# Cached-attention decode block: one in-order load queue with a rotating ring in place of two queues with two slots each, and another route for the probabilities

## The chip, the cores and the metric

The kernel runs on one core of a Trainium2 chip. The metric is the device time of one execution in microseconds. Before the change three executions took 1314.25, 1317.78 and 1319.87 us; the median is 1317.78 us. The profile is of the first of these, with a span of 1312.3 us from its first to its last instruction.

A core has five engines that run their own instruction streams and meet at semaphores: PE (TensorE, matmul), DVE (VectorE), ACT (ScalarE), POOL (GpSimd) and SP (SyncE). Loads from memory are issued by SP and ACT and carried by the core's 16 DMA engines.

## The reference, cut to what matters

One token for each of 4 sequences goes through an attention block with a cache of 8192 keys and values for each of 32 heads, and then through a gated MLP. Both sit behind a layer norm and a residual.

```python
B, Sq, D = 4, 1, 512
H, Sk, Dh = 32, 8192, 128
...
q = (layernorm(x) @ wq).reshape(B, Sq, H, Dh).transpose(0, 2, 1, 3)
scores = einsum("bhqd,bhkd->bhqk", q, k_cache) * (Dh ** -0.5)
p = softmax(scores, axis=-1)
o = einsum("bhqk,bhkd->bhqd", p, v_cache)
h = x + o.transpose(0, 2, 1, 3).reshape(B, Sq, H * Dh) @ wo
# gated MLP, F = 1792
hn = layernorm(h)
h2 = h + (sigmoid(hn @ w_gate) * (hn @ w_up)) @ w_down
```

All arrays are bf16. The key cache and the value cache are 4 x 32 x 8192 x 128 x 2 bytes = 268 MB each; the weights come to some 14 MB.

## The kernel before

The 128 pairs of sequence and head are the steps of the kernel (NST = 128). One load brings a tile of two heads of K, or of V: 4096 KB, so 64 tiles of each (NT2 = 64). Eight steps make a group (GS = 8, so NG = 16) with one softmax. The values are used LAG = 10 steps behind the keys. A ring of NS = 4 slots in on-chip memory holds the tiles.

**Slots and queues.** K owns slots 0 and 1, V owns slots 2 and 3. At the start slot 3 holds wq, and slot 2 holds a scratch form of the queries ("qr"). `place` notes which tile last held the slot (`prev_of`); a load waits until that tile is `consumed`.

```python
        owner = [None, None, ("qr", 0), None]
        ...
        place(("wq", 0), 3)
        for t in range(NT2):
            place(("k", t), t % 2)
            place(("v", t), 2 + t % 2)
        place(("wg", 0), 0)
        slot_of[("wu", 0)], prev_of[("wu", 0)] = 0, prev_of[("wg", 0)]
        place(("wd", 0), 1)
        ...
        for it in [("wq", 0)] + [("k", t) for t in range(NT2)] + [("wg", 0), ("wu", 0), ("wd", 0)]:
            issue("sp", it)
```

**Keys.** Four VectorE transposes a step turn the tile half of one head (as uint32, 128 x 1024 each), and 16 matmuls add the scores to the group's bank. After its second step a K tile is consumed.

```python
        def dve_T(s):
            ...
                    return e.transpose(kT[:, buf, i * q:(i + 1) * q].bitcast(U32),
                                       ringv(src)[:, base + i * q:base + (i + 1) * q].bitcast(U32))
                op = P("dve", f, [dma_of[it][0], sc_of.get(s - 2)])
            ...
            consumed[it] = op
```

**Softmax of a group.** VectorE takes the row maximum of the scores (`chain_mx`, step 8 after the group's first), PE and VectorE bring it to one row and back (`chain_p1`, `chain_d2`, `chain_p2`, steps 8 and 9), and ScalarE takes the exponential into `E_sb` (128 x 512, bf16) with its sums (`chain_exp`, step 9).

**Probabilities to the key partitions.** This is the first part that the change touches. 64 matmuls of 32 columns each, with a block of `E_sb` as the stationary operand, put the probabilities into a PSUM bank with the keys on the partitions; two ScalarE copies then spread them into `PTz`, a zero-padded tile.

```python
        def chain_pt(g):
            def f(e):
                for rr in range(16):
                    for a in range(4):
                        mm = e.matmul(bP[g % 2][32 * a:32 * (a + 1), 32 * rr:32 * rr + 32],
                                      E_sb[:, 32 * rr:32 * rr + 32], Sel[:, a, :], start=True, stop=True,
                                      tile_position=(0, 32 * a))
                return mm
            pt_of[g] = P("pe", f, [exp_of[g], c_sel] + list(ptc_of.get(g - 2, ())))
            ...
                    src = bP[g % 2][p0:p0 + 64, :].rearrange("p (q r m) -> p q m r", q=4, r=4)
                    return e.activation(dst, src, ACT.Copy)
                ops.append(P("act", fc, [pt_of[g], zp] + last_pv))
```

**Values.** 16 matmuls of 128 x 512 a step take `PTz` as the stationary operand and the V tile as the moving one. They wait for the group's `PTz` and the V tile. A V tile is consumed after its second step.

**Order of a step.** On VectorE a step's four transposes come first, with the softmax pieces between or behind them. On PE come the scores of step s, the pieces of the softmax, the values of step s - 10, and then `chain_pt` where s is 9 past a group's first step. The next V load and, near the end, the eight loads of wo stand on ScalarE at the end of a step:

```python
            t = (s - LAG - 1) // 2 + 2
            if (s - LAG) % 2 == 1 and 2 <= t < NT2:
                for i in wo_after.get(t, ()):
                    issue("act", ("wo", i))
                issue("act", ("v", t))
```

**The end.** wo lies over the buffer of the transposed keys, so its loads wait for the last scores. The last V tile comes in three pieces. Then follow the sum's scaling, the product with wo, the second norm, gate and up (one 1792 KB load each), the hidden vector `hh_sb`, and down (three pieces, 5, 5 and 4 of 14 row blocks), and 4 KB of output. The loads of w_gate, w_up and w_down wait for the values of step 123 too:

```python
        for it, ops in dma_of.items():
            for op in ops:
                op.deps = [sc_of[NST - 1]] if it[0] == "wo" else [consumed[p] for p in prev_of[it]]
                if it[0] in ("wg", "wu", "wd"):
                    op.deps.append(pv_of[NST - 5])
```

Of the kernel before, what the change touches and what calls it, by code (L numbers as in the profile page):

```python
# [5 lines left out]
BF16 = mybir.dt.bfloat16  # L6
# [3 lines left out]
ACT = mybir.ActivationFunctionType  # L10
# [5 lines left out]
LAG = 10  # L16
NS = 4
# [57 lines left out]
def bass_sequential_preLN__mha_block_cached__glu_gated_glu__decode_kernel(  # L75
# [12 lines left out]
    B, _sq, D = A_x.shape  # L88
# [7 lines left out]
    NT2 = NT // 2  # L96
    NST = NT
    NG = NST // GS
    R = S // 64
    TW = R * 128  # L100
# [6 lines left out]
    P = prog.add  # L107

    with ExitStack() as es:
        def SB(name, shape, dt):  # L110
            return es.enter_context(nc.sbuf_tensor(name, shape, dt))
# [12 lines left out]
        Sel = SB("Sel", [128, 4, 32], BF16)  # L124
        SelQ = SB("SelQ", [128, 4, 4], BF16)
# [8 lines left out]
        xT = SB("xT", [128, NDC * B], FP32)  # L134
        xnT = SB("xnT", [128, NDC, 32], BF16)
        E_sb = SB("E_sb", [128, 512], BF16)
        PZ0 = 24
        PTz = SB("PTz", [128, 2, 128 * 32 + 32], BF16)
        mx = SB("mx", [128, 1], FP32)
# [18 lines left out]
        bS, bO, bP = bank[0:2], bank[2:4], bank[4:6]  # L158
        bX, bH = bank[6], bank[7]
# [8 lines left out]
        def ringv(slot):  # L168
            return ring[:, slot, :]
# [2 lines left out]
        VL_PARTS = [(0, 64), (64, 96), (96, 128)]  # L172
        NWO = 8
        HW = H // NWO

        slot_of, prev_of, dma_of, uses = {}, {}, {}, [0] * NS
        owner = [None, None, ("qr", 0), None]

        def place(it, slot):
            slot_of[it] = slot  # L180
            prev_of[it] = [owner[slot]] if owner[slot] is not None else []
            owner[slot] = it
        place(("wq", 0), 3)
        for t in range(NT2):
            place(("k", t), t % 2)
            place(("v", t), 2 + t % 2)
        place(("wg", 0), 0)
        slot_of[("wu", 0)], prev_of[("wu", 0)] = 0, prev_of[("wg", 0)]
        place(("wd", 0), 1)
        consumed = {}  # L190

        wq_v = ring[:, slot_of[("wq", 0)], :].rearrange("p (c f) -> p c f", c=NDC)
# [5 lines left out]
        def kv_src(t, cache):  # L198
# [4 lines left out]
                  sem=s_x, val=16)  # L203
# [40 lines left out]
                dst, src = wu_v, B_w_up.rearrange("(c p) f -> p c f", p=128)  # L244
            return [(lambda e: e.dma_start(dst, src).then_inc(sem, 16), sem, val)]  # L245

        def issue(eng, it):
            dma_of[it] = [P(eng, fn, (), sem, val) for fn, sem, val in load(it)]


        for it in [("wq", 0)] + [("k", t) for t in range(NT2)] + [("wg", 0), ("wu", 0), ("wd", 0)]:
            issue("sp", it)


        def pool(fn, deps=()):
# [70 lines left out]
        consumed[("wq", 0)] = p_q[1]  # L326


        QR0 = 2 * TW
        q_ev = []  # L330
        for half in range(2):
            for a in range(4):
# [9 lines left out]
        def pe_qT(e, half):  # L342
            mm = None
            for h in range(16 * half, 16 * half + 16):
                j = (h // 4) % 4
                for v in range(4):
                    off = half * 2048 + ((h % 4) * 4 + v) * 128
                    c0 = ((h * 4) + v) * 4
                    mm = e.matmul(bX[:, c0:c0 + B], ringv(2)[:, off:off + 128], SelQ[:, j, 0:B], start=True, stop=True)
# [6 lines left out]
        for b in range(B):  # L356
            ops = []
# [22 lines left out]
        z_of, ot_of, otc_of = {}, {}, {}  # L380

        def dve_T(s):
            it = ("k", s // 2)
            src, buf, base = slot_of[it], s % 2, (s % 2) * HT
            q = HT // 4
            op = None
            for i in range(4):
                def f(e, i=i):
# [3 lines that stand above are left out]
                yield  # L392
            T_of[s] = op
            consumed[it] = op
# [82 lines left out]
            d3_of[g] = P("dve", lambda e: e.reciprocal(rinv[:, g % 2:g % 2 + 1], bX[:, 0:1]), [L_of[g], z_of.get(g - 2)])  # L477

        def chain_pt(g):
            def f(e):  # L480
                mm = None
                for rr in range(16):
                    for a in range(4):
                        mm = e.matmul(bP[g % 2][32 * a:32 * (a + 1), 32 * rr:32 * rr + 32],  # L484
                                      E_sb[:, 32 * rr:32 * rr + 32], Sel[:, a, :], start=True, stop=True,
                                      tile_position=(0, 32 * a))
                return mm
            pt_of[g] = P("pe", f, [exp_of[g], c_sel] + list(ptc_of.get(g - 2, ())))
            last_pv = [pv_of[(g - 2) * GS + GS - 1]] if g >= 2 else []
            ops = []  # L490
            for h2 in range(2):
                def fc(e, h2=h2):
                    p0 = 64 * h2

                    dst = bass.AP(PTz, p0 * 2 * 4128 + (g % 2) * 4128 + PZ0 + 4 * h2,
                                  [[2 * 4128, 64], [1024, 4], [32, 32], [1, 4]])
                    src = bP[g % 2][p0:p0 + 64, :].rearrange("p (q r m) -> p q m r", q=4, r=4)
                    return e.activation(dst, src, ACT.Copy)  # L498
                ops.append(P("act", fc, [pt_of[g], zp] + last_pv))
            ptc_of[g] = ops  # L500

        def chain_z(g):
# [14 lines left out]
        def hook(s, base):  # L517
            g = (s - base) // GS
            return g if (s - base) % GS == 0 and 0 <= g < NG else None

        issue("act", ("v", 0))
        issue("act", ("v", 1))
        wo_after = {NT2 - 3: (0, 1), NT2 - 2: (2, 3, 4), NT2 - 1: (5, 6, 7)}


        for s in range(NST + LAG - 2 + 4):
            tr = dve_T(s) if s < NST else iter(())
            for i in range(4):
# [36 lines left out]
            if g is not None and g < NG - 1:  # L565
                chain_ot(g)
            t = (s - LAG - 1) // 2 + 2
            if (s - LAG) % 2 == 1 and 2 <= t < NT2:
                for i in wo_after.get(t, ()):
                    issue("act", ("wo", i))  # L570
                issue("act", ("v", t))


        def wo_mms(e, heads, b0, b1, first=False):
# [8 lines left out]
        gl = NG - 1  # L583
        P("pe", lambda e: wo_mms(e, range(0, H - 8), 0, B, True), [otc_of[gl - 1], dma_of[("wo", NWO - 1)][0], d_xnT])
        if B > 1:
# [15 lines left out]
                                          start=True, stop=True), [d_hsq, c_mean, d3_of[gl]])  # L601
# [45 lines left out]
        p_o = P("pe", lambda e: e.matmul(bP[0][0:NB, 0:128], oT[:, :], ident[:, :], start=True, stop=True),  # L647
                [d_o] + list(ptc_of[gl]) + list(ptc_of[gl - 1]))
        o0 = P("dve", lambda e: e.tensor_copy(o_sb[:, :], bP[0][0:NB, 0:128]), [p_o])
        consumed[("wg", 0)] = consumed[("wu", 0)] = consumed[("wd", 0)] = p_d[-1]  # L650

# [2 lines left out]
            return e.wait_ge(s_out, 16)  # L654
        P("sp", sp_out, [o0])

        for it, ops in dma_of.items():
            for op in ops:
                op.deps = [sc_of[NST - 1]] if it[0] == "wo" else [consumed[p] for p in prev_of[it]]
                if it[0] in ("wg", "wu", "wd"):  # L660
                    op.deps.append(pv_of[NST - 5])

        prog.resolve(sems)
        with nc.Block() as block:
# [47 lines left out]
```

## Time and profile before

| | before |
|---|---|
| median of three executions | 1317.78 us |
| span of the profiled one | 1312.3 us |
| read from memory | 550.77 MB, 420 GB/s over the span |
| VectorE busy | 625.6 us, of which the K transposes 588.2 us |
| PE busy | 473.4 us, mean granted clock 0.649 |
| ScalarE busy | 46.0 us |
| K load, issue to landing | 29.6 us, median of 64 |
| V load, issue to landing | 32.2 us, median of 63 |

How to read the profile. Its first part gives the busy time of each engine, its share of the span and the number of instructions; PEld is the weight load of PE. The second part cuts the span into 40 equal slices of 32.8 us: a digit is the busy share in tenths, and GB/s is what the DMA engines moved. The third lists the queues: packets, megabytes, and the share of the 16 engines' time. Windows give the same for any stretch in us from the span's start: its length, then the busy time (and instructions) of PE, PEld, DVE, ACT and POOL, then the granted clock of PE, the DMA share and GB/s. A window of a few us carries an error of some GB/s, since whole packets are counted. The chain of waits follows the work that ended last back to its start: the start of a piece, its length, and what it was. A DMA piece lasts from its issue to its landing.

### The profile page before, as it was taken

To read this page: it belongs to the slowest core of one execution; us is meant where nothing else is said; L and a number is where in the kernel's file an instruction comes from. 1 tells how busy PE (TensorE), PEld (TensorE's weight loads), DVE (VectorE), ACT (ScalarE), POOL (GpSimd) and SP (SyncE) were. 2 spreads that over 40 slices of the span, in tenths; PEclk is the share of its full clock that TensorE was granted. 3 is DMA by queue.
4 is the path that set the end of the run, shared out by engine and by line. 5 is a ranking of instruction groups with operands and counts; after the bars stand their busy time and mean duration, and the time that the engine had idled before them with its cause. 6 is when DMAs were issued, how large, how long until landed. Compare 5 with 4: busy or idle time off the path is not lost.

```text
span 1312.3 us, 12694 instructions
## 1 busy us (share of the span) xinstructions
PE 473.4 (36%) x5827; PEld 176.8 (13%) x5827; DVE 625.6 (48%) x641; ACT 46.0 (4%) x102; POOL 10.6 (1%) x22
## 2 busy tenths in 40 slices
PE   2134342333333253332334244243243234323324
PEld 1011110111111010110111011011111111111113
DVE  5486455445355355445446445445535436545300
ACT  2000000000000000000000000000000000000000
POOL 3000000000000000000000000000000000000000
PEclk9997556775566656676665655676556665577665
DMA  9999999999999999999999999999999999999895
GB/s 402 432 380 418 434 430 432 430 431 429 430 432 430 431 430 432 431 430 431 429 431 432 431 431 432 431 430 432 428 432 431 430 430 431 431 430 430 356 396 209
DMA packets 26076, 551.58 MB, mean 420 GB/s; under 512 B 2340, under 2 KB 8232, under 8 KB 9256
## 3 DMA queue, kind: packets, MB, share of 16 engines
q1 hardware_dynamic: 12288, 278.14, 49.6%
q10 hardware_dynamic: 13736, 272.64, 48.7%
q8 instruction: 45, 0.74, 0.2%
q14 instruction: 7, 0.06, 0.0%
HBM read 550.77 MB, written 0.00 MB: 420 GB/s over the span
## 4 chain that ended last, share of the span: by engine, by line
DMA 71%; DVE 24%; ACTq 3%; PE 1%; issue 1%; ACT 0%; DVEq 0%
DMA ring<-in_A_k_cache_dram 66%; DVE kT L389 22%; DMA ring<-in_A_v_cache_dram 3%; ACTq L209 2%; DMA ring<-in_A_wq_dram 1%; ACTq L217 1%; DVE mx L445 1%; ACTq L245 0%; PE PS L322 0%; DVE Lq L366 0%; DVE rowx L457 0%; PE PS L624 0%; PE PS L431 0%; DVE mrow L455 0%; DVE ring L339 0%
## 5 line engine op out<-in xcount | busy, mean ns | idle before, releaser
L389 DVE STREAM_TRANSPOSE kT<-ring 128x1024 uint32<-128x1024 uint32 x512 | 588.2, 1209 | 591.1 <-DMA ring<-in_A_k_cache_dram 591.1
L407 PE MATMUL PS<-kT,Lq 128*32 128x512 bf16 x2048 | 217.6, 566 | 773.5 <-DVE kT L389 606.5
L431 PE MATMUL PS<-ring,PTz 128*32 128x512 bf16 x2048 | 210.1, 553 | 33.9 <-DMA ring<-in_A_v_cache_dram 33.6
L407 PEld LDWEIGHTS PS<-kT,Lq 128*32 128x32 bf16 x2048 | 53.9, 119 | 914.8 <-DVE kT L389 673.0
L431 PEld LDWEIGHTS PS<-ring,PTz 128*32 128x32 bf16 x2048 | 64.8, 125 | 132.8 <-issue 81.0
L466 ACT ACTIVATE negm<-PS 128x1 f32<-128x1 f32 x16 | 2.7, 171 | 1157.2 <-PE PS L462 1157.2
L503 DVE TENSOR_SCALAR Zs<-PS,rinv 128x512 f32<-128x512 f32 x16 | 11.6, 724 | 49.4 <-PE PS L431 49.4
L498 ACT ACTIVATE PTz<-PS 64x512 bf16<-64x512 f32 x32 | 18.9, 591 | 18.5 <-PE PS L484 18.1
L510 PE MATMUL PS<-SelZ,Zs 128*128 128x8 f32 x128 | 18.2, 269 | 0.9 <-DVE Zs L503 0.9
L510 PEld LDWEIGHTS PS<-SelZ,Zs 128*128 128x128 f32 x128 | 16.7, 204 | 10.2 <-issue 8.4
L484 PEld LDWEIGHTS PS<-Sel,E_sb 128*32 128x32 bf16 x1024 | 11.3, 100 | 9.1 <-ACT E_sb L468 6.7
L484 PE MATMUL PS<-Sel,E_sb 128*32 128x32 bf16 x1024 | 11.4, 188 | 1.5 <-ACT E_sb L468 1.1
L445 DVE TENSOR_REDUCE mx<-PS 128x1 f32<-128x512 f32 x16 | 10.5, 657 | 1.3 <-PE PS L407 1.2
L468 ACT ACTIVATE E_sb<-PS,negm 128x512 bf16<-128x512 f32 x16 | 11.0, 687 | 0.5
L473 PEld LDWEIGHTS PS<-sig,Gsum 128*128 128x128 f32 x32 | 7.8, 305 | 12.6 <-issue 12.6
L515 DVE CAST OT<-PS 128x8 bf16<-128x8 f32 x16 | 2.1, 132 | 15.5 <-PE PS L510 15.5
L473 PE MATMUL PS<-sig,Gsum 128*128 128x1 f32 x32 | 9.2, 356 | 0.0
L578 PE MATMUL PS<-OT,kT 128*128 128x4 bf16 (+2 forms) x160 | 4.6, 167 | 11.3 <-DMA kT<-in_A_wo_dram 11.0
L462 PE MATMUL PS<-onesf,rowx 1*128 1x1 f32 x32 | 7.5, 300 | 0.0
L462 PEld LDWEIGHTS PS<-onesf,rowx 1*128 1x128 f32 x32 | 6.1, 237 | 9.8 <-issue 9.8
L339 DVE CAST ring<-PS 128x512 bf16<-128x512 f32 x4 | 2.5, 684 | 9.8 <-PE PS L322 9.8
L578 PEld LDWEIGHTS PS<-OT,kT 128*128 128x128 bf16 x160 | 4.4, 103 | 12.2 <-issue 11.9
(78 smaller groups left out, 77.1 us busy)
## 6 DMA issues: line engine op xcount, KB each, us to landing
ring<-in_A_k_cache_dram SPq DMA_DIRECT2D x64, 4096.0 KB, 29.6
ring<-in_A_v_cache_dram ACTq DMA_DIRECT2D x63, 4096.0 KB, 32.2
ring<-in_A_wq_dram SPq DMA_DIRECT2D x1, 4096.0 KB, 12.2
kT<-in_A_wo_dram ACTq DMA_DIRECT2D x8, 512.0 KB, 18.8
ring<-in_A_v_cache_dram ACTq DMA_DIRECT2D x1, 2048.0 KB, 28.3
ring<-in_A_v_cache_dram ACTq DMA_DIRECT2D x2, 1024.0 KB, 21.8
ring<-in_B_w_gate_dram SPq DMA_DIRECT2D x1, 1792.0 KB, 16.2
ring<-in_B_w_up_dram SPq DMA_DIRECT2D x1, 1792.0 KB, 21.8
```

What stands on the lines that cost most here:

```text
L209: return [(lambda e: e.dma_start(wo_v[:, HW * t:HW * t + HW, :], A_wo.rearrange("(h p) f -> p h f", p=128)[:, HW * t:HW * t + HW, :]).then ...
L217: return e.dma_start(ringv(slot)[:, c0:c1], kv_src(t, A_v_cache)[:, c0:c1]).then_inc(s_piece[i], 16)
L389: return e.transpose(kT[:, buf, i * q:(i + 1) * q].bitcast(U32), ringv(src)[:, base + i * q:base + (i + 1) * q].bitcast(U32))
L407: mm = e.matmul(bS[g % 2][32 * j:32 * (j + 1), :], Lq[:, l0:l0 + 32], rhs, start=(s % GS == 0 and v == 0), stop=(s % GS == GS - 1 and v == 3),
L431: mm = e.matmul(bO[g % 2][32 * rq:32 * (rq + 1), :], PTz[:, g % 2, l0:l0 + 32], ringv(slot)[:, r0 * 128:(r0 + 4) * 128], start=(s % GS == ...
L445: mx_of[g] = P("dve", lambda e: e.tensor_reduce(mx[:, :], bS[g % 2][:, :], AX.X, ALU.max), [sc_of[g * GS + GS - 1], p1_of.get(g - 1)])
L462: p2_of[g] = P("pe", lambda e: e.matmul(bX[:, 0:1], rowx[0:1, :], onesf[0:1, 0:1], start=True, stop=True), [d2b_of[g], c_ones])
L473: L_of[g] = P("pe", lambda e: e.matmul(bX[:, 0:1], Gsum[:, :], sig[:, 0:1], start=True, stop=True), [exp_of[g], a1_of[g], d_g])
L484: mm = e.matmul(bP[g % 2][32 * a:32 * (a + 1), 32 * rr:32 * rr + 32], E_sb[:, 32 * rr:32 * rr + 32], Sel[:, a, :], start=True, stop=True, ...
L498: return e.activation(dst, src, ACT.Copy)
L503: z_of[g] = P("dve", lambda e: e.tensor_scalar(Zs[:, :], bO[g % 2][:, :], rinv[:, g % 2:g % 2 + 1], None, op0=ALU.mult), [pv_of[g * GS + G ...
L510: mm = e.matmul(bX[:, 256:264], Zs[:, 128 * r:128 * (r + 1)], SelZ[:, r, :], start=(r == 0), stop=(r == 3))
```

## The change

It has two parts.

The first puts every load on SyncE, in one list: wq, then the first five K tiles, then K and V in turn with V five tiles behind, wo in three portions between the last V tiles, and gate, up and down behind the last V. The slots go round in the order of this list, whatever the kind. It is for a fixed order of the loads, which is the order of use, and it takes the DMA issues and their waits off ScalarE. The extra wait of the last weights is dropped.

The second changes how the probabilities come to the key partitions. Four matmuls of 512 columns gather the rows of `E_sb` (with a selection matrix as the stationary operand), ScalarE copies the result to `Ep`, VectorE transposes it in 32 x 32 blocks to `Et` at the start of the next step, and the two ScalarE copies spread `Et` into `PTz`. It is for fewer PE instructions, and it needs one PSUM bank in place of two.

```diff
+        Ep = SB("Ep", [128, 512], BF16)
+        Et = SB("Et", [128, 512], BF16)
 ...
-        owner = [None, None, ("qr", 0), None]
-        def place(it, slot):
 ...
-        for t in range(NT2):
-            place(("k", t), t % 2)
-            place(("v", t), 2 + t % 2)
 ...
+        LAG2 = LAG // 2
+        items = [("wq", 0)]
+        for t in range(NT2 + LAG2):
+            if t < NT2:
+                items.append(("k", t))
+            if t >= LAG2:
+                items.append(("v", t - LAG2))
+            for i in {LAG2 - 4: (0, 1), LAG2 - 3: (2, 3, 4), LAG2 - 2: (5, 6, 7)}.get(t - NT2, ()):
+                items.append(("wo", i))
+        items += [("wg", 0), ("wu", 0), ("wd", 0)]
+        owner = [None] * (NS - 1) + [("qr", 0)]
+        cur = 0
+        for it in items:
 ...
+            slot_of[it] = cur
+            prev_of[it] = [owner[cur]] if owner[cur] is not None else []
+            owner[cur] = it
+            cur = (cur + 1) % NS
 ...
-        for it in [("wq", 0)] + [("k", t) for t in range(NT2)] + [("wg", 0), ("wu", 0), ("wd", 0)]:
-            issue("sp", it)
+        for it in items:
+            dma_of[it] = [P("sp", fn, (), sem, val) for fn, sem, val in load(it)]
 ...
         def chain_pt(g):
-                for rr in range(16):
-                    for a in range(4):
-                        mm = e.matmul(bP[g % 2][32 * a:32 * (a + 1), 32 * rr:32 * rr + 32],
-                                      E_sb[:, 32 * rr:32 * rr + 32], Sel[:, a, :], start=True, stop=True,
-                                      tile_position=(0, 32 * a))
+                for a in range(4):
+                    mm = e.matmul(bP[0][32 * a:32 * (a + 1), :], Sel[:, a, :], E_sb[:, :], start=True, stop=True,
+                                  tile_position=(0, 32 * a))
-            pt_of[g] = P("pe", f, [exp_of[g], c_sel] + list(ptc_of.get(g - 2, ())))
+            pt_of[g] = P("pe", f, [exp_of[g], c_sel, epc_of.get(g - 1)])
+            epc_of[g] = P("act", lambda e: e.activation(Ep[:, :], bP[0][:, :], ACT.Copy), [pt_of[g], et_of.get(g - 1)])
+
+        def chain_et(g):
+            et_of[g] = P("dve", lambda e: e.transpose(Et[:, :], Ep[:, :]), [epc_of[g]] + list(ptc_of.get(g - 1, ())))
 ...
-                    src = bP[g % 2][p0:p0 + 64, :].rearrange("p (q r m) -> p q m r", q=4, r=4)
+                    src = Et[p0:p0 + 64, :].rearrange("p (q r m) -> p q m r", q=4, r=4)
 ...
-        issue("act", ("v", 0))
-        issue("act", ("v", 1))
-        wo_after = {NT2 - 3: (0, 1), NT2 - 2: (2, 3, 4), NT2 - 1: (5, 6, 7)}
         for s in range(NST + LAG - 2 + 4):
+            g = hook(s, 10)
+            if g is not None:
+                chain_et(g)
 ...
-                if it[0] in ("wg", "wu", "wd"):
-                    op.deps.append(pv_of[NST - 5])
```

With the rotation the query scratch moves to slot 3, wq to slot 0; K tiles come to slots 1, 2, 3, 0, 1, 2, and from k6 and v1 on K alternates between slots 0 and 2 and V between 1 and 3.

More of the change, by code (lines that the diff above doesn't have):

```diff
@@ L174, in bass_sequential_preLN__mha_block_cached__glu_gated_glu__decode_kernel @@
         HW = H // NWO
-        slot_of, prev_of, dma_of, uses = {}, {}, {}, [0] * NS
-        owner = [None, None, ("qr", 0), None]
-        def place(it, slot):
[L180 to L183, printed above, removed]
-        for t in range(NT2):
-            place(("k", t), t % 2)
-            place(("v", t), 2 + t % 2)
-        place(("wg", 0), 0)
-        slot_of[("wu", 0)], prev_of[("wu", 0)] = 0, prev_of[("wg", 0)]
-        place(("wd", 0), 1)
+        LAG2 = LAG // 2
[8 more added lines that the diff above has]
+        items += [("wg", 0), ("wu", 0), ("wd", 0)]
+        slot_of, prev_of, dma_of = {}, {}, {}
+        owner = [None] * (NS - 1) + [("qr", 0)]
+        uses = [0] * NS
+        cur = 0
+        for it in items:
+            if it[0] == "wo":
+                continue
+            if it[0] == "wu":
+                slot_of[it], prev_of[it] = slot_of[("wg", 0)], prev_of[("wg", 0)]
+                continue
+            slot_of[it] = cur
+            prev_of[it] = [owner[cur]] if owner[cur] is not None else []
+            owner[cur] = it
+            cur = (cur + 1) % NS
         consumed = {}
@@ L245, in load @@
             return [(lambda e: e.dma_start(dst, src).then_inc(sem, 16), sem, val)]
-        def issue(eng, it):
-            dma_of[it] = [P(eng, fn, (), sem, val) for fn, sem, val in load(it)]
-        for it in [("wq", 0)] + [("k", t) for t in range(NT2)] + [("wg", 0), ("wu", 0), ("wd", 0)]:
-            issue("sp", it)
+        for it in items:
+            dma_of[it] = [P("sp", fn, (), sem, val) for fn, sem, val in load(it)]
         def pool(fn, deps=()):
@@ L326, in bass_sequential_preLN__mha_block_cached__glu_gated_glu__decode_kernel @@
         consumed[("wq", 0)] = p_q[1]
-        QR0 = 2 * TW
+        QR0 = (NS - 1) * TW
         q_ev = []
@@ L348, in pe_qT @@
                     c0 = ((h * 4) + v) * 4
-                    mm = e.matmul(bX[:, c0:c0 + B], ringv(2)[:, off:off + 128], SelQ[:, j, 0:B], start=True, stop=True)
+                    mm = e.matmul(bX[:, c0:c0 + B], ringv(NS - 1)[:, off:off + 128], SelQ[:, j, 0:B], start=True, stop=True)
             return mm
@@ L379, in bass_sequential_preLN__mha_block_cached__glu_gated_glu__decode_kernel @@
         mx_of, d2_of, exp_of, pt_of, ptc_of, L_of, d3_of = {}, {}, {}, {}, {}, {}, {}
-        z_of, ot_of, otc_of = {}, {}, {}
+        z_of, ot_of, otc_of, epc_of, et_of = {}, {}, {}, {}, {}
         def dve_T(s):
@@ L496, in fc @@
                                   [[2 * 4128, 64], [1024, 4], [32, 32], [1, 4]])
-                    src = bP[g % 2][p0:p0 + 64, :].rearrange("p (q r m) -> p q m r", q=4, r=4)
+                    src = Et[p0:p0 + 64, :].rearrange("p (q r m) -> p q m r", q=4, r=4)
                     return e.activation(dst, src, ACT.Copy)
-                ops.append(P("act", fc, [pt_of[g], zp] + last_pv))
+                ops.append(P("act", fc, [et_of[g], zp] + last_pv))
             ptc_of[g] = ops
@@ L566, in bass_sequential_preLN__mha_block_cached__glu_gated_glu__decode_kernel @@
                 chain_ot(g)
[L567 to L571, printed above, removed]
         def wo_mms(e, heads, b0, b1, first=False):
@@ L647, in bass_sequential_preLN__mha_block_cached__glu_gated_glu__decode_kernel @@
         p_o = P("pe", lambda e: e.matmul(bP[0][0:NB, 0:128], oT[:, :], ident[:, :], start=True, stop=True),
-                [d_o] + list(ptc_of[gl]) + list(ptc_of[gl - 1]))
+                [d_o, epc_of[gl]])
         o0 = P("dve", lambda e: e.tensor_copy(o_sb[:, :], bP[0][0:NB, 0:128]), [p_o])
@@ L655, in bass_sequential_preLN__mha_block_cached__glu_gated_glu__decode_kernel @@
         P("sp", sp_out, [o0])
-        for it, ops in dma_of.items():
-            for op in ops:
+        for it in items:
+            for op in dma_of[it]:
                 op.deps = [sc_of[NST - 1]] if it[0] == "wo" else [consumed[p] for p in prev_of[it]]
-                if it[0] in ("wg", "wu", "wd"):
-                    op.deps.append(pv_of[NST - 5])
         prog.resolve(sems)
```

## The prediction

> **What bounds the kernel now.** I read the page first: engines, slices, queues.
>
> ```profile
> PE 473.4 (36%) x5827; PEld 176.8 (13%) x5827; DVE 625.6 (48%) x641; ACT 46.0 (4%) x102; POOL 10.6 (1%) x22
> DMA  9999999999999999999999999999999999999895
> GB/s 402 432 380 418 434 430 432 430 431 429 430 432 430 431 430 432 431 430 431 429 431 432 431 431 432 431 430 432 428 432 431 430 430 431 431 430 430 356 396 209
> ...
> q1 hardware_dynamic: 12288, 278.14, 49.6%
> q10 hardware_dynamic: 13736, 272.64, 48.7%
> ```
>
> No engine is busy for half of the span, and the DMA digits are 9 nearly throughout. The rate row says more: 428 to 434 GB/s in every slice from the fifth to the 37th, whatever the engines do. The two queues together move 551 MB; at 431 GB/s that is 1279 us of a span of 1312.3 us. So only some 33 us can be had without moving fewer bytes or moving them faster, and they must lie in the slow slices: the first four and the last three. Next I asked for those stretches in windows of 10 us and 6 us (last two columns: DMA share and GB/s).
>
> ```profile
> 60.00:70.00 10.00, 2.26 (x20) 0.59 (x24) 9.13 (x8) 0.00 (x0) 0.00 (x0) 1.00 0.97 419
> 70.00:80.00 10.00, 3.44 (x32) 0.75 (x24) 7.41 (x7) 0.00 (x0) 0.00 (x0) 1.00 1.00 403
> 80.00:90.00 10.00, 4.10 (x33) 0.98 (x33) 9.40 (x10) 0.00 (x0) 0.00 (x0) 1.00 0.86 338
> 90.00:100.00 10.00, 4.55 (x98) 2.00 (x98) 8.69 (x10) 2.13 (x5) 0.00 (x0) 1.00 0.91 367
> 100.00:110.00 10.00, 5.36 (x58) 1.83 (x50) 7.00 (x8) 0.00 (x0) 0.00 (x0) 0.89 0.98 398
> ```
>
> ```profile
> 1220.00:1226.00 6.00, 2.89 (x28) 1.08 (x32) 6.00 (x6) 0.00 (x0) 0.00 (x0) 0.50 0.67 289
> 1226.00:1232.00 6.00, 4.12 (x59) 1.51 (x51) 2.74 (x5) 0.00 (x0) 0.00 (x0) 0.89 0.54 188
> 1232.00:1238.00 6.00, 2.08 (x84) 1.24 (x83) 0.82 (x2) 2.13 (x5) 0.00 (x0) 0.97 1.03 436
> ```
>
> Last, the chain that ended last, for the end of the span (start, length, what):
>
> ```profile
> 1274.31 22.60 DMA ring<-in_A_v_cache_dram
> ...
> 1304.47 3.16 PE PS L624 x112
> ...
> 1307.99 1.67 PE PS L638 x56
> ...
> 1310.24 0.28 DVE o_sb L649
> ```
>
> The three places are now plain. **Start:** V0 and V1 fill their two slots and stay there until step 10 (LAG), so K alone keeps the DMA going, and with two K slots each new K load is issued only when a tile has been transposed (its 8 transposes take VectorE 9.1 us in the timeline). A lone 4 MiB load took 12.65 us from issue to landing (69.61 to 82.27), against 9.73 us that 4.19 MB takes at 431 GB/s: some 2.9 us of latency shows. **Last group:** K63 lands at 1218.5, and both V slots wait for the softmax chain of the last group while K has nothing more to load. **End:** the last piece of V lands at 1296.9, no bytes follow, and 15.4 us of dependent arithmetic run with an idle DMA.
>
> **What the Trainium skill says.** "DMA: Bandwidth & Descriptors", section "Issuing engines are not separate DMA queues": loads started by SyncE and ScalarE run on the same 16 engines, and a second issuer saves only issue time. The trace agrees as far as it goes: a K or V issue takes SyncE or ScalarE 0.33 us, beside 9.73 us of data. Section "Where 436 GB/s comes from" of that page puts the ceiling at 435 GB/s; 431 measured is 99% of it, so the steady state has no more to give. Section "Queues, rings and completion order": each DMA engine takes a ring's descriptors in order, and alternates by packets between queues that have work. In this trace a K load takes 29.6 us from issue to landing, three tile times, since it shares the engines with V. "VectorE: DVE Perf Modes", section "The three transpose paths": the VectorE transpose works in separate 32x32 blocks, which is what lets one instruction finish the new probability layout; no trace of before shows this shape.
>
> **The change, part 1: one in-order queue.** All loads move to SyncE, in the order k5, v0, k6, v1, ..., and slots are handed out in rotation. In the steady state K keeps two slots and V two, so each load still waits for the tile two before it of its own kind. Is that slack enough? Tiles land every 9.73 us. K(t) lands at 0, is transposed by about 10, and its slot's next tile should start flowing at 29 (three other loads lie between). That is some 19 us of slack, and about 2.9 us of latency comes off it. V(t) is used by two value steps of 1.9 us each and is free some 5 us after landing. So two to three loads are always queued, and I expect 431 GB/s as before. Does one queue reach that rate? Before 22.6 us only SyncE's queue is active: 10 to 20 us shows 436 GB/s. And K1 landed at 41.0: with about 2.9 us of latency at the head, three tiles alone would have ended at 32.1; V0's data began at about 24.6, so the remaining 7.5 us double to 15, giving 39.6 plus the landing. That leaves no room for a single queue more than a few per cent slower.
>
> Start: k0 and k1 go at once; k2 waits for the q work (done at 21.2), k3 for wq, k4 for k0's transposes (34.9) while k2 and k3 flow until about 52; v0 waits for k2's transposes. Always something is queued. Against 431, the four windows from 70 to 110 us lack 28 + 93 + 64 + 33 = 218 GB/s over 10 us each: 218 x 10 / 431 = **5.1 us** regained.
>
> Last group: after k63, the loads v58, v59 and v60 are already in line, 29 us of data. The chain of the last group takes 1218.5 to 1235 here, 16.5 us. The hole of (142 + 243) x 6 / 431 = **5.4 us** closes.
>
> End: the weights come last, behind V63, and flow during the arithmetic. They are 5.5 MB; at about 400 GB/s (this stretch of small rows showed 363 to 436) 13.8 us. From the last V landing the arithmetic to the hidden vector takes 1307.95 - 1296.92 = 11.0 us, less than that. After the last w_down piece remain 16 of the 56 matmuls of 1.67 us, 0.5 us, and from 1309.66 to the end 2.6 us: 3.1 us in place of 15.4, a gain of **12.3 us**.
>
> **Part 2: the probability path.** Per group it takes out 64 small matmuls (0.70 us) and adds 4 matmuls of 128x512 (16 of that shape took 1.05 us at full clock, 1.9 at half, so about 0.3 to 0.5), a ScalarE copy of 128x512 from PSUM (0.60 by L338), and a VectorE transpose of 512 bf16 columns. The last is an estimate from the K transposes: 1.2 us for 1024 elements a row, so 0.6. The two ScalarE copies of 0.59 stay. Per group the chain grows by about 1 us, ScalarE and VectorE by 0.6 us each, 10 us over 16 groups. The new thing is a wait on VectorE: at the start of step 10 of a group it waits for scores, exp, the gather and the copy, 5 to 7 us with the value matmuls in front of it. K tiles come 19.5 us apart and need 9.7, so this fits into its idle time (591 us waiting for K). Worth on the path: 0.
>
> Sum: 1312.3 - 5.1 - 5.4 - 12.3 = 1289.5 us of span. The median time lies 5.5 us over the profiled span (1317.8 against 1312.3), so **1295 us**, 1.7% less.
>
> **Rivals.** (A) One queue streams worse than two, because at the seam of two loads nothing else fills an engine. Each 0.1 us lost at 130 seams costs 13 us: 0.2 us would eat all the gain, and the time would be about 1318. For it: lone loads show 2.9 us of latency. Against it: loads are queued ahead, and the early windows. (B) The in-order queue blocks at its head: one late slot stops the loads of both kinds, and VectorE's wait now ties K's release to V's landing. If the slack were used up, some us per group would go, 16 x 3 = 48 us, giving 1340. Against it: 19 us of slack. (C) The wo loads hurt: before, ScalarE was held 13.7 us by three of their issues (1239.3 to 1253). Held SyncE cannot send the next V; three seams of 2 us would take back 6 us, giving 1301. (D) The single queue runs a little better, at 434, with no alternation: 9 us less, 1286.
>
> **Range and chances.** My middle is 1295; D and a better end reach 1283, C with half of A reaches 1312. The line of 2% is 1291.4, close under my middle: faster by over 2%: 0.34; within 2%: 0.59; slower by over 2%, from A or B: 0.07.
>
> **What would show it.** Right: the GB/s row at 430 or more from the second slice to the last but one; no low window near 80 or 1225; the chain near the end going through w_down and not through V, with 3 us after its landing; the K transposes still ending their idle time on K's DMA. Wrong: a steady rate under 428 (A), K transposes idle on the Et transpose or SyncE's waits followed by low windows every 78 us (B), dips between V60 and V63 (C), over 8 us after the last landing.

## The result and the profile after

The changed kernel takes **1295.22 us** (median; 1295.11 to 1295.36), against 1316.43 us for the kernel before in the same comparison: a ratio of 0.9837, 95% interval 0.9813 to 0.986. The prediction was 1295. The profiled span is 1293.4 us against 1312.3, so 18.9 us went.

The page of the changed kernel first: the DMA digits, the rate by slices (each now 32.3 us), the queues.

```profile
DMA  9999999999999999999999999999999999999998
GB/s 405 432 428 433 433 427 433 431 430 434 427 431 432 429 431 432 432 428 433 432 430 429 433 429 431 431 432 431 431 429 432 431 429 434 430 430 431 428 382 322
...
q1 hardware_dynamic: 26016, 550.78, 99.5%
...
q10 hardware_dynamic: 8, 0.00, 0.0%
```

The whole load is now on one queue, at the same 431 GB/s in the middle. The slow slices at the start are gone, but for the first. At the end, two slices are still slow, and they are now slow with a DMA digit of 9 or 8, not of 5.

The windows of the start, in the form used before:

```profile
60.00:70.00 10.00, 4.10 (x33) 0.98 (x33) 9.38 (x10) 0.00 (x0) 0.00 (x0) 0.50 0.99 424
70.00:80.00 10.00, 3.03 (x23) 1.06 (x22) 5.12 (x7) 2.53 (x5) 0.00 (x0) 0.50 1.00 429
80.00:90.00 10.00, 6.19 (x54) 2.18 (x58) 8.05 (x9) 1.17 (x2) 0.00 (x0) 0.50 1.03 441
90.00:100.00 10.00, 3.55 (x32) 0.75 (x24) 7.75 (x7) 0.00 (x0) 0.00 (x0) 0.67 1.00 429
```

The dip to 338 is gone. Over the first 140 us the mean rate is 426 GB/s, against 410 before: 16 x 140 / 431 = 5.2 us. The last group, in windows of 6 us (the last two columns are DMA share and GB/s):

```profile
1218.00:1224.00 6.00, 1.60 (x29) 0.54 (x17) 1.18 (x3) 0.00 (x0) 0.00 (x0) 1.00 0.99 426
1224.00:1230.00 6.00, 4.75 (x39) 1.72 (x39) 0.00 (x0) 0.98 (x4) 0.00 (x0) 0.56 1.04 421
1230.00:1236.00 6.00, 1.36 (x14) 0.82 (x18) 1.41 (x3) 4.17 (x5) 0.00 (x0) 0.50 1.02 406
1236.00:1242.00 6.00, 3.60 (x36) 1.77 (x28) 0.17 (x1) 0.00 (x0) 0.00 (x0) 0.78 0.96 385
1242.00:1248.00 6.00, 0.19 (x4) 0.14 (x8) 0.00 (x0) 0.00 (x0) 0.00 (x0) 0.50 0.82 290
```

The hole behind the last K load (DMA shares of 0.67 and 0.54, 4.7 us of idle engines) is closed; a smaller one, 1.3 us by its shares of 0.96 and 0.82, stands where wo is loaded. The end of the chain of waits:

```profile
1277.91 12.20 DMA ring<-in_B_w_down_dram
1290.10 0.05 issue
1290.15 0.60 PE PS L645 x16
1290.75 0.02 issue
1290.77 0.20 DVE oT L651
```

What the arithmetic waits for last is now w_down and no longer V. It lands at 1290.1, and 3.3 us later all is done; before, 15.4 us followed the landing of the last V. That V was not the last load to land, though. The last piece of w_down was still under way on SyncE's queue (its three issues, with the start of the first and of the last; then, of the list of loads, the last piece with its time to landing):

```profile
L225 SPq DMA_DIRECT2D ring<-in_B_w_down_dram x3: 505/6005/12228, 1260.9 to 1273.7; - x3
```

```profile
ring<-in_B_w_down_dram SPq DMA_DIRECT2D x1, 512.0 KB, 25.1
```

It landed at 1273.7 + 25.1 = 1298.8, 1.9 us after V, and nothing waited for it then. So the last landing of all moved from 1298.8 to 1290.1, by 8.7 us, and what follows it went from 13.5 to 3.3 us.

### The profile page after: what moved, and what is told of

Read it like the earlier page. It is cut to its first block, busy times and chain, and to the rows that moved or that the text cites. A ratio compares the mean times of both kernels' runs of the same rounds, so it can differ in the third digit from the quotient of the medians.

```text
span 1293.4 us, 10805 instructions
## 1 busy us (share of the span) xinstructions
PE 494.7 (38%) x4867; PEld 183.3 (14%) x4867; DVE 636.9 (49%) x657; ACT 70.7 (5%) x118; POOL 10.7 (1%) x22
## 4 chain that ended last, share of the span: by engine, by line
DMA 80%; PE 12%; SPq 4%; DVE 3%; issue 0%; ACT 0%
DMA ring<-in_A_v_cache_dram 76%; PE PS L441 7%; PE PS L417 4%; SPq L222 2%; DMA ring<-in_A_k_cache_dram 2%; DVE kT L399 2%; SPq L238 1%; DMA ring<-in_A_wq_dram 1%; DMA ring<-in_B_w_down_dram 1%; SPq L230 1%; SPq L258 0%; PE PS L332 0%; DVE Lq L376 0%; DVE ring L349 0%; PE PS L359 0%
## 5 line engine op out<-in xcount | busy, mean ns | idle before, releaser
L399 DVE STREAM_TRANSPOSE kT<-ring 128x1024 uint32<-128x1024 uint32 x512 | 587.9, 1209 | 480.9 <-DMA ring<-in_A_k_cache_dram 480.9
L417 PE MATMUL PS<-kT,Lq 128*32 128x512 bf16 x2048 | 241.3, 619 | 570.1 <-DVE kT L399 447.8
L441 PE MATMUL PS<-ring,PTz 128*32 128x512 bf16 x2048 | 215.6, 566 | 205.3 <-DMA ring<-in_A_v_cache_dram 205.3
L417 PEld LDWEIGHTS PS<-kT,Lq 128*32 128x32 bf16 x2048 | 69.0, 136 | 705.4 <-DVE kT L399 481.6
L502 DVE STREAM_TRANSPOSE Et<-Ep 128x512 bf16<-128x512 bf16 x16 | 11.4, 712 | 97.4 <-ACT Ep L498 97.4
L511 ACT ACTIVATE PTz<-Et 64x512 bf16<-64x512 bf16 x32 | 34.0, 1062 | 12.8 <-DVE Et L502 12.5
L498 ACT ACTIVATE Ep<-PS 128x512 bf16<-128x512 f32 x16 | 9.6, 597 | 11.3 <-PE PS L494 11.3
L494 PE MATMUL PS<-E_sb,Sel 128*32 128x512 bf16 x64 | 7.0, 429 | 1.9 <-ACT E_sb L478 1.3
L332 PE MATMUL PS<-ring,xnT 128*32 128x512 bf16 x32 | 3.5, 615 | 6.6 <-DMA ring<-in_A_wq_dram 6.6
## 6 DMA issues: line engine op xcount, KB each, us to landing
ring<-in_A_wq_dram SPq DMA_DIRECT2D x1, 4096.0 KB, 12.3
```

The lines of the kernel that those rows point to most:

```text
L417: mm = e.matmul(bS[g % 2][32 * j:32 * (j + 1), :], Lq[:, l0:l0 + 32], rhs, start=(s % GS == 0 and v == 0), stop=(s % GS == GS - 1 and v == 3),
L441: mm = e.matmul(bO[g % 2][32 * rq:32 * (rq + 1), :], PTz[:, g % 2, l0:l0 + 32], ringv(slot)[:, r0 * 128:(r0 + 4) * 128], start=(s % GS == ...
L502: et_of[g] = P("dve", lambda e: e.transpose(Et[:, :], Ep[:, :]), [epc_of[g]] + list(ptc_of.get(g - 1, ())))
```

## The experiments

**Part 2 alone** (`e1_prob_only`): the kernel before with the row gathering, the copy and the block transpose.

```diff
 kernel before
-  64 matmuls of 32 columns -> PSUM -> PTz
+  4 matmuls of 512 columns -> PSUM -> Ep -> (VectorE transpose) Et -> PTz
```

> The kernel before with the new probability path alone (row gathering, copy, block transpose), loads left on two queues. My theory (the loads set the time, the path of the probabilities lies beside them): a ratio of 1.00, within 0.4%, some 1316 us, with the hole after the last K load up to 1.5 us longer since the last group's chain is longer. Rival (the new wait on VectorE, or the fewer PE instructions, is worth something on the path): a ratio of 0.995 or less if it is where some of the gain comes from, 1.01 or more if it costs 1 us in each of the 16 groups.

Measured: 1316.86 us against 1314.66, ratio 1.0011 (1.0004 to 1.0018). The ratio makes it 1.4 us and the medians 2.2, so the new path costs one to two us there, and brings nothing. Its rate by slices (of an execution with a span of 1315.3 us, 3.0 over the profiled one of before) shows where:

```profile
GB/s 402 436 375 367 430 431 430 431 434 429 431 433 432 432 431 431 430 431 431 431 431 432 431 430 432 431 432 429 431 431 431 432 431 432 432 432 431 360 397 207
```

The fourth slice fell from 418 to 367, and the middle is untouched. VectorE's timeline there (start, length, what; in brackets the idle time before it and what ended it):

```profile
90.43 2.35 DVE L391 STREAM_TRANSPOSE kT<-ring 128x1024 uint32<-128x1024 uint32 x2
97.62 0.71 DVE L494 STREAM_TRANSPOSE Et<-Ep 128x512 bf16<-128x512 bf16 x1 [4.84 <-ACT Ep L490]
98.26 9.09 DVE L391 STREAM_TRANSPOSE kT<-ring 128x1024 uint32<-128x1024 uint32 x8
```

With two K slots, K's release is on the path at the start, and there VectorE's wait for the copy Ep holds it up; from 100 to 110 us the DMA moves only 211 GB/s. Neither theory had this place.

**Part 1 alone** (`e2_queue_only`): the changed kernel with the 64 small matmuls put back.

```diff
 changed kernel
-  4 matmuls of 512 columns -> PSUM -> Ep -> (VectorE transpose) Et -> PTz
+  64 matmuls of 32 columns -> PSUM -> PTz
```

> The changed kernel with the old probability path (64 small matmuls, no block transpose), loads in one queue. My theory: all of the change's gain is here, ratio 0.984, some 1295 us, equal to the changed kernel within 2 us. Rival (the block transpose's wait on VectorE ties the release of K to the landing of V and costs something): 3 us or more below the changed kernel. Rival (the new path brings part of the gain): 3 us or more above it.

Measured: 1296.33 us, ratio 0.9862 (0.9846 to 0.9878). Its interval overlaps that of the changed kernel (0.9813 to 0.986), so all of the gain that can be told from zero is in the loads. In this order the wait on VectorE (97.4 us in the changed kernel, 16 times) costs nothing that shows. It lies in VectorE's waiting for K: here that is 578.5 us, in the changed kernel 480.9 for K and 97.4 for Ep, 578.3 together. At the start, where it cost something on two slots, K now has more of them; the rate over the first 140 us is 425 GB/s here and 426 in the changed kernel.

**The weights ahead of the last V** (`e3_weights_before_v63`).

```diff
-        items += [("wg", 0), ("wu", 0), ("wd", 0)]
+        items[-1:] = [("wg", 0), ("wu", 0), ("wd", 0), items[-1]]
```

> The changed kernel with the three MLP weights loaded just ahead of the last V tile, not behind it; the same bytes in the same single queue. My theory (the end gains because 5.5 MB flow under the last arithmetic): the idle tail of about 15.4 us after the last landing is back in place of 3.3, so the span grows by about 12 us to 1305, ratio 0.993. Rival (the gain at the end comes from the single queue or from better use of the DMA, not from what is loaded last): no more than 3 us above the changed kernel.

Measured: 1307.02 us, ratio 0.9943 (0.9928 to 0.9958), 11.8 us over the changed kernel. The chain of waits:

```profile
1275.00 15.19 DMA ring<-in_A_v_cache_dram
...
1296.91 3.16 PE PS L631 x112
...
1300.43 1.67 PE PS L645 x56
```

The last landing is at 1290.2, within 0.1 us of the changed kernel's, but now it is V's, and the span ends 14.6 us after it. The same bytes in the same time: only what lands last has changed.

**The end alone, on two queues** (`e4_two_queues_weights_last`): before, with the weights on ScalarE's queue behind V63.

```diff
-        for it in [("wq", 0)] + [("k", t) for t in range(NT2)] + [("wg", 0), ("wu", 0), ("wd", 0)]:
+        for it in [("wq", 0)] + [("k", t) for t in range(NT2)]:
             issue("sp", it)
 ...  # behind the last V on ScalarE
+        for it in [("wg", 0), ("wu", 0), ("wd", 0)]:
+            issue("act", it)
```

> The kernel before with one thing moved: the three MLP weights are issued by ScalarE behind the last V tile, on the queue of V, in place of SyncE's queue beside it. Two queues and two slots each stay. My theory: the end of the change alone, 12 us less, some 1305 us, ratio 0.991, with the slow windows near 80 us and in the last group still there. Rival (a single queue for everything is what counts): ratio 1.00, within 0.3%. Against me: ScalarE may be held by full queues while the second norm needs it, which would cost 1 to 3 us.

Measured: 1305.04 us, ratio 0.9929 (0.9914 to 0.9943), 9.3 us, and both earlier slow places are still there. No single queue is needed for this part. It is 3 us short of the 12. w_down lands at 1287.68 + 12.20 = 1299.9. Against the last V of the kernel before, at 1296.9, that is 3.0 us later; but there w_down itself landed at 1298.8, so 1.9 of them were never to be had by a change of order. For the other 1.1 the start and the hole are enough, which were slower in this execution (408 GB/s over the first 140 us and 5.5 us of idle engines, against 410 and 4.7; 1.4 us together).

**The start alone, on two queues** (`e5_two_queues_rotation`): before, with slots handed out in rotation.

```diff
+        cur = 0
+        for it in items:      # k0..k4, then k, v in turn
+            slot_of[it] = cur; prev_of[it] = [owner[cur]] if owner[cur] is not None else []
+            owner[cur] = it; cur = (cur + 1) % NS
 ...  # K stays on SyncE, V on ScalarE
-        issue("act", ("v", 0)); issue("act", ("v", 1))
+            if s in (5, 9):
+                issue("act", ("v", (s - 5) // 4))
```

> The kernel before with the rotating slots of the change, but K still on SyncE's queue and V on ScalarE's; the first two V tiles are issued after steps 5 and 9, the weights as before. It gives K four slots at the start and changes nothing else. My theory: the slow windows between 70 and 110 us go away and 5 us are gained, ratio 0.996; the hole in the last group stays (it comes from V running ahead of its order of use on its own queue), and so does the idle tail of 15 us. Rival (a fixed order in one queue is what fills the start): ratio 1.00.

Measured: 1307.18 us, ratio 0.9933 (0.9919 to 0.9946), 8.9 us by the medians and 7.2 by the spans. More than expected. The first 140 us run at 426 GB/s as in the changed kernel, which is the 5.2 us. The rest is in the hole:

```profile
1224.00:1230.00 6.00, 3.61 (x34) 1.43 (x38) 0.00 (x0) 0.95 (x3) 0.00 (x0) 0.57 0.70 302
1230.00:1236.00 6.00, 1.69 (x74) 1.30 (x66) 0.82 (x2) 1.18 (x2) 0.00 (x0) 0.50 0.87 327
```

It is there, but with shares of 0.70 and 0.87, 2.6 us of idle engines against 4.7. I read it so: K has the DMA to itself for five tiles at the start, V is that much further behind, and more of it is left to load when K ends (K63 lands at 1210.3 here, at 1218.5 before). No run separates this from other effects of the rotation.

**Start and end on two queues** (`e8_two_queues_both`): the edits of the last two runs together.

```diff
+  rotation of slots, V0 and V1 after steps 5 and 9   (as in the run above)
+  w_gate, w_up, w_down on ScalarE behind V63           (as in the run before it)
```

> Two queues as before, with rotating slots (K has four at the start) and with the MLP weights on ScalarE's queue behind the last V tile: the gains of start and end without the single queue. My theory: 5 and 12 us, 17 us in all, some 1299 us, ratio 0.987; what is left to the changed kernel is the hole of the last group, 5 us, which needs the fixed order of K and V. Rival (the hole also comes from the late weights or the slots): equal to the changed kernel, 0.984. Rival (the single queue is what counts): 0.995 or more.

Measured: 1296.76 us, ratio 0.9854 (0.984 to 0.9867). That is the single queue with the same probability path (`e2_queue_only`, 1296.33 us, 0.9862) within the intervals; the last bytes land at 1291.7 and 1291.1. And it is the time at which the last bytes land in `e5_two_queues_rotation`, where V63 lands at 1289.7 and the last piece of w_down, beside it on the other queue, at 1266.7 + 25.0 = 1291.7:

```profile
L237 SPq DMA_DIRECT2D ring<-in_B_w_down_dram x3: 507/6006/12524, 1253.6 to 1266.7; - x3
```

```profile
ring<-in_B_w_down_dram SPq DMA_DIRECT2D x1, 512.0 KB, 25.0
```

So the loads take the same time with the weights beside V and behind it. I had given the single queue 5 us for the hole, and it shows no gain in time that can be told from zero. In the traces the hole is 2.7 us of idle engines here (shares of 0.68 and 0.87 from 1224 to 1236 us) and 1.3 us in `e2_queue_only` (0.78 from 1242 to 1248), so about a microsecond may still be the queue's. What the change brings is an order of slots and of last loads; the number of queues has almost no part in it.

**Four loads a tile** (`e6_split4`), for rival A, the seams.

```diff
+NP = 4
 ...
+            if kind in ("k", "v"):
 ...
+                cw = TW // NP
+                return [(lambda e, c=c: e.dma_start(ringv(slot)[:, c * cw:(c + 1) * cw],
+                                                    kv_src(t, cache)[:, c * cw:(c + 1) * cw]).then_inc(sem, 16), sem, val)
+                        for c in range(NP)]
```

> The changed kernel with each K and V load cut into four loads of 1024 KB, so that there are some 510 seams in the one queue in place of 130. My theory (seams cost nothing as long as more loads are queued): steady rate 431 GB/s as before, time within 3 us of the changed kernel, ratio 0.984. Rival (each seam of a lone queue leaves the engines idle for a moment): 380 more seams at 0.05 us are 19 us, at 0.1 us 38 us, and the steady rate falls to 425 or 419 GB/s.

Measured: 1324.01 us, ratio 1.0059 (1.0043 to 1.0074), the steady rate 421 GB/s. By these numbers the rival was right, at 0.08 us a seam (28.8 us over 380 seams). But the cut also made each row 8 KB in place of 32 KB. So:

**Two loads a tile, the same short rows** (`e10_two_loads_short_rows`).

```diff
+                dst = ringv(slot).rearrange("p (c a x) -> p a c x", c=2, a=2)
+                src = kv_src(t, cache).rearrange("p (c a x) -> p a c x", c=2, a=2)
+                return [(lambda e, i=i: e.dma_start(dst[:, i, :, :], src[:, i, :, :]).then_inc(sem, 16), sem, val)
+                        for i in range(2)]
```

> The changed kernel with each K and V tile brought by two loads of 2048 KB, the first with the first and third quarter of every row, the second with the others: rows of 8 KB as in the run with four loads (there 421 GB/s), but one extra seam a tile in place of three. If the number of rows sets the rate: 421 GB/s again, some 1322 us, ratio 1.005. If the seams of the single queue set it (0.079 us each by the run with four loads, 9.73 us a tile without): 9.81 us a tile, 428 GB/s, some 1305 us, ratio 0.992.

Measured: 1323.75 us, ratio 1.0069 (1.0054 to 1.0084). Its page:

```profile
GB/s 395 420 422 421 421 421 421 422 421 421 421 422 421 421 422 420 422 421 421 422 421 422 421 420 422 422 421 422 420 421 421 421 421 421 422 421 420 421 379 329
DMA packets 76870, 551.48 MB, mean 417 GB/s; under 512 B 4372, under 2 KB 10264, under 8 KB 11288
```

Again 421, with a third of the extra seams, and 76870 packets where the changed kernel has 26069. The rows count, not the seams: rival A is out. A tile takes 4.194 MB / 421 = 9.96 us in place of 9.73, and each of the 16 engines moves 32 rows for it in place of 8, so a row costs some 0.23 us / 24 = 9.6 ns on top of its bytes.

That number reads the end of the changed kernel. wo has rows of 1 KB, 32 an engine in each of its eight loads. In PE's timeline the value steps start with the landing of V60, V61 and V62, at 1235.1, 1247.8 and 1261.9. Between the first two lie V61 and two wo loads: 9.73 + 2.43 + 64 x 0.0096 = 12.8 us, and 12.7 were taken. Between the next, V62 and three: 14.3, and 14.1 were taken. So short rows are enough for this spacing. They are not all of the lowest window: from 1242 to 1248 us, 290 GB/s are 2.0 us of data less than 431 would be, and by the share of 0.82 the engines are idle for 1.1 of these.

**wo on the other queue** (`e7_wo_act`).

```diff
         for it in items:
-            dma_of[it] = [P("sp", fn, (), sem, val) for fn, sem, val in load(it)]
+            if it[0] != "wo":
+                dma_of[it] = [P("sp", fn, (), sem, val) for fn, sem, val in load(it)]
 ...  # on ScalarE, after the last group's PTz
+        for i in range(NWO):
+            dma_of[("wo", i)] = [P("act", fn, (), sem, val) for fn, sem, val in load(("wo", i))]
```

> The changed kernel with the eight wo loads issued by ScalarE, on its own queue, after the last group's probabilities are spread; SyncE issues V60 to V63 without being held by them. My theory (the low window of 290 GB/s at 1242 to 1248 us in the changed kernel comes from SyncE being held for 23.3 us by three wo issues, so that V62 is issued late): the low window closes and 2 us are gained, ratio 0.982. Rival (the low rate belongs to the small rows of wo, wherever they are issued): the same time as the changed kernel within 0.5 us, with the lost rate spread over other windows.

Measured: 1313.08 us, ratio 0.9974 (0.9964 to 0.9985): 18 us lost, and neither theory was near. The low window did close (424 GB/s at 1242 to 1248), and the last byte landed at 1289.6, only 0.5 us sooner than in the changed kernel. But it was wo's. ScalarE's timeline and then the chain of waits:

```profile
1231.22 1.51 ACTq L222 DMA_DIRECT2D kT<-in_A_wo_dram  x3
...
1232.76 46.18 ACTq L222 DMA_DIRECT2D kT<-in_A_wo_dram  x5
```

```profile
1276.29 13.33 DMA kT<-in_A_wo_dram
1289.75 3.55 PE PS L589 x128
```

4.2 MB of wo took from 1231 to 1290, 58 us, while V61, V62, V63 and the weights went by. The packets in this trace show why: the two queues go row for row. From 1235 to 1245 us, 123 rows of 32 KB start on SyncE's queue and 137 rows of 1 KB on ScalarE's; from 1250 to 1280 us, where SyncE's rows become shorter, 2537 and 2582. So a 1 KB row of wo is answered by a row of V of 32 KB, and wo moves at a small part of the rate. That fits the Trainium skill ("DMA: Bandwidth & Descriptors", section "Queues, rings and completion order"), which has an engine change between queues after each packet; where it speaks of some 9 to 17 descriptors (single moves) in a packet, the turn here is one row. The attention output needs wo before the arithmetic behind it, so all that follows comes late.

**Longer rows for w_down** (`e11_down_rows`).

```diff
-    B_w_down.rearrange("(t p) f -> p t f", p=128)      wv[:, c, 128 * t:128 * (t + 1)]
+    B_w_down.rearrange("(p t) f -> p t f", p=128)      wv[:, c, t:F:NFT]
```

> The changed kernel with w_down laid out so that a partition holds 14 neighbouring rows of it (one load row is 4 to 5 KB in place of 1 KB); gate and up take their columns with a step of 14 to match. The same bytes, the same result. w_down is the last to land in the changed kernel. If small rows are what keeps the last stretch under 431 GB/s (5.5 MB in the 13.9 us from the last V to the last w_down piece, 396 GB/s), it lands about 1 us sooner: some 1294 us, ratio 0.983. Rival (the low rate there is drain and latency, or the stepped weight reads cost PE more than is gained): no gain, or up to 2 us more.

Measured: 1297.19 us, ratio 0.9866 (0.985 to 0.9883): the rival. In the chain of waits w_down is gone and gate and up stand in its place:

```profile
1283.55 6.90 PE PS L631 x112
...
1290.54 0.22 DVE hh_sb L637
...
1290.81 1.67 PE PS L645 x56
```

The 112 matmuls took 6.9 us against 3.2 in the changed kernel: with columns 28 bytes apart a weight load takes 161 ns in place of 104, and PE becomes what ends last. The rows did come sooner: the last piece of w_down lands at 1273.4 + 15.9 = 1289.3, 0.8 us before that of the changed kernel, close to the 1 us expected. So that part of my theory held, and the cost on PE was larger. Not all of the low rate is rows: in both kernels the DMA share falls well under 1 from 1284 to 1290 us, to 0.58 in the changed one and to 0.39 here.

**fp32 on the probability path** (`e9_f32_path`).

```diff
-        Ep = SB("Ep", [128, 512], BF16); Et = SB("Et", [128, 512], BF16)
+        Ep = SB("Ep", [128, 512], FP32); Et = SB("Et", [128, 512], FP32)
```

> The changed kernel with Ep and Et in fp32 in place of bf16. It looks at one thing: the two copies into PTz take 1062 ns from Et where they took 591 ns from PSUM with the same pattern. If the 2-byte source with its step of 64 bytes is what slows them, they fall back towards 0.6 us with a 4-byte source; if it is the memory they read from, they stay near 1.06 us. The time should not move: within 2 us of the changed kernel.

Measured: 1295.57 us in one execution. The copies into PTz, in the kernel before, in the changed kernel behind its transpose, and here (count, then busy us and mean ns of one):

```profile
L498 ACT ACTIVATE PTz<-PS 64x512 bf16<-64x512 f32 x32 | 18.9, 591 | 18.5 <-PE PS L484 18.1
```

```profile
L502 DVE STREAM_TRANSPOSE Et<-Ep 128x512 bf16<-128x512 bf16 x16 | 11.4, 712 | 97.4 <-ACT Ep L498 97.4
L511 ACT ACTIVATE PTz<-Et 64x512 bf16<-64x512 bf16 x32 | 34.0, 1062 | 12.8 <-DVE Et L502 12.5
```

```profile
L511 ACT ACTIVATE PTz<-Et 64x512 bf16<-64x512 f32 x32 | 34.5, 1077 | 12.8 <-DVE Et L502 12.4
```

At 1077 ns, the element size is not what made the copies slower. The copies here and in the kernel before read the same type in the same pattern and write the same tile; what differs is the memory that they read, PSUM at 591 ns and SBUF at 1077. That is shown for this stepped pattern alone, since no run varied it.

No version here beats the changed kernel.

## Why the prediction was right, and where it was not

The mechanism was right: the loads at 431 GB/s set the time, the steady state could not move, and the gain lay at start, last group and end. The total was right partly by luck. The sum gave a span of 1289.5 and it is 1293.4, so the gain was put 3.9 us too high. Against that, I put the median 5.5 us over the span, from the kernel before; here it lies 1.8 us over. Of the 5.5 us only 2.0 belong to an execution (1314.25 us with a span of 1312.3); the rest is that the profiled execution was the fastest of three. The two errors nearly cancel.

- **Start, 5.1 us:** 5.2 by the rate over the first 140 us, and `e5_two_queues_rotation` has the same rate by rotation alone.
- **Last group, 5.4 us:** too large, and put down to the wrong part. Idle engine time fell from 4.7 to 1.3 us, 3.4 us. And 2.1 of these come with the rotation on two queues. "The hole closes" held; the in-order queue was not what mainly closed it.
- **End, 12.3 us:** as a swap of 15.4 for 3.3 us it held (12.1), and so did the 13.8 us for the weights (V63's last matmuls start at 1276.3, w_down lands at 1290.1). What failed is the step "no bytes follow": behind the last V, at 1296.9, the last piece of w_down was still to land, at 1298.8. A new order of the same bytes could not bring the end of the loads back to where V had landed, so 1.9 us of the 12.3 were not there. Counted from the last landing of all, the end gave 13.5 - 3.3 = 10.2 us.
- These account for the span: 5.2 + 3.4 + 10.2 = 18.8 of 18.9 us. The first two, 8.6 us, are also what the last landing moved by, 8.7.
- **Part 2, worth 0:** right in the changed kernel. In the kernel before it cost one to two us, at the start. The sizes: the four gathering matmuls 0.64 us, the copy 0.60, the block transpose 0.71 (estimated 0.6), but the two spreading copies 1.06 each, which I had left at 0.59.
- **Steady state:** 431 GB/s before and after. The ceiling of 435 GB/s that the prediction sets beside it is that of the fabric; the section that it names in the Trainium skill ("DMA: Bandwidth & Descriptors", section "Where 436 GB/s comes from") says that a transfer between memory and SBUF is held lower, at about 358 GB/s. This kernel measured 431, so that lower figure did not hold here, and that the steady state has no more to give rests on the runs and not on the page.
- **Rivals:** A fell with `e10_two_loads_short_rows`; B fell with `e2_queue_only` and with the slices from the second to the 38th, all at 427 to 434 GB/s; D fell, the rate is 431. C, SyncE held by wo, is visible (23.3 us for three issues, and the low window between V60 and V63), but its price is at most the 1.3 us of idle engines, and moving wo elsewhere cost far more.

## What to carry to other kernels

When the DMA runs at its limit for nearly all of a kernel, look for the gain only where its rate dips, and decide what lands last: weights with little work behind them, and not the tile with a long chain behind it. Before you price that, find the last landing on every queue: the chain of waits names only the load that was waited for. Ask then which rows are short: they cost engine time, and on a queue of their own they crawl as long as a queue of long rows runs beside them. A change of queues can look like the cause when it is the order of slots that came with it: test the order with the queues left alone.

## What the runs showed of the hardware that I had not expected

- A row cost some 9.6 ns on an engine beyond its bytes: 431 GB/s with 32 KB rows, 421 with 8 KB rows, whether a tile came in two loads or in four.
- Two queues took turns row by row (123 rows of 32 KB and 137 of 1 KB in the same 10 us), so 4.2 MB in 1 KB rows took 58 us on a second queue.
- A ScalarE copy of 64 x 512 with the same stepped pattern took 591 ns from PSUM (fp32) and from on-chip SBUF memory 1062 ns in bf16 and 1077 in fp32.
- Weight loads with columns 28 bytes apart took 161 ns against 104.
